# Sliding-window attention into a softplus MLP on one core: PSUM tiles of one bank in turn in place of halves of a two-bank tile, with a new hand-written opening order

## The chip, the cores and the metric

The kernel runs on one core of one Trainium2 chip. The metric is the device time of one execution in microseconds (us). It was 723.93 us before the change, the median of three runs (721.24 to 726.59).

## The reference

Attention over 4 batches, 8 heads, 768 positions of 64 dimensions, with a causal window of 128 positions and 4 positions at the start of the sequence (sinks) that all later positions see; its output feeds a two-layer MLP.

```python
scores = scale * np.matmul(q, k.transpose(0, 1, 3, 2))
keep = is_sink | in_window            # key < 4, or 0 <= query - key < 128
scores = np.where(keep, scores, -1000000000.0)
scores = scores - np.max(scores, axis=-1, keepdims=True)
a = np.exp(scores)
a = a / (np.sum(a, axis=-1, keepdims=True) + 1e-09)
out = np.matmul(a, v).astype(np.float32)
...
x = out.transpose(0, 2, 1, 3).reshape(B * S, H * D)       # 3072 x 512
h = x @ w_in                                              # w_in 512 x 2048
g = np.maximum(h, 0.0) + np.log1p(np.exp(-np.abs(h)))
return (g @ w_out).astype(np.float32)                     # w_out 2048 x 512
```

## The kernel before

**Work and tiling.** The 3072 tokens are 12 chunks of 256 (two blocks of 128 queries). For each chunk there are 8 heads of attention, and then the MLP of the chunk in 8 blocks of 256 hidden columns. The MLP of a chunk runs 8 heads behind its attention, so a steady step is one head of one chunk beside one MLP block of the chunk before it. MLP blocks are numbered over all chunks here: U9 is the second block of chunk 1, U17 the second of chunk 2, U33 the second of chunk 4. Heads likewise: S47 is the last head of chunk 5.

Chunks 0 and 1 are "exact": their heads go in pairs, in plain fp32. All later products split each operand into a high part and the rest, so that one product becomes two or three matmuls (tile names that end in h and l).

**The steps**, each a letter of the order: S scores (L245 for a pair, L260 and L261 for a head), T softmax (DVE L277 or L282 copies the diagonal, DVE L289 adds the mask and takes the maximum, ACT L290 exponentiates), N normalise (L303, L304, then L308 or L315), W transposes of the weights (PE L351 or L373, then a copy and two selections on POOL), k and K the sinks' weights (DVE L320, PE L331), V values (PE L395 and L402, or L414 and L420), O the head's output with its high part xh and rest xl (L432, L433, or L438 to L443). For the MLP: U is 24 matmuls of 128x256 (L551), F softplus in three ACT passes (L558 Abs, L559 Exp, L560 Ln), P the gate (DVE L566 reads the product in PSUM again and writes mt; then a copy to gh), R the residue (DVE, gl = mt - gh), D and E the second product, 6 matmuls each of 128x512 (L588 to L590) into the two acc tiles. The weights arrive as 64-bit words: w is the DMA of half a block (L456), a a cast of the upper word, c the assembled float (DVE L491), d its high part, l its low part (a subtraction at L67, on DVE or POOL). There are 32 halves: wi and wo for each of the 8 blocks, two halves each. L and G load q, k and v by SP's queue (L195 or L200, and L220); p and q split them; j, J and Y are the sinks of the values.

**What sets the order.** Inside `_fast` every engine runs its instructions in program order. The order is a list of tokens written by hand, `Ctx.START` (up to U9: chunks 0 and 1, the weights, the first blocks), and after it `Ctx.STEADY`, two strings of letters, one for most heads and one for the first head of a chunk. The strings `NM`, `TH`, `GH`, `WT`, `WH`, `WL` choose the engine of the n-th normalise, copy or weight step; their last letter holds for all that come later. SP's queue issues its DMAs in program order too, so an issue that waits holds all behind it.

**PSUM.** [...] Four tiles matter. `sb` (L933, two banks) holds scores: in a pair one bank for each head, later one bank for each block j. `hb` (two banks) holds the product of U: its halves, one bank each, alternate by `turn_h` (L545, L546). In chunk 0 the second block of a pair also uses it (L241). `xb` (one bank) holds values. `acc0` and `acc1` are the outputs, one bank each; one bank is for transposes. sb, hb and xb are each a single tile for the whole program, and the halves are slices of it. Waits between engines are made per tile: the framework that places them sees accesses to tiles.

Of the kernel before, what the change touches and what calls it, by code (L numbers as in the profile page):

```python
# [11 lines left out]
F32 = mybir.dt.float32  # L12
# [53 lines left out]
def _sub(nc, eng, out, a, b):  # L66
    (nc.vector if eng == "V" else nc.gpsimd).tensor_tensor(out, a, b, ALU.subtract)  # L67
# [64 lines left out]
class _Attention:  # L132
# [103 lines left out]
    def pair_scores(self, h, j):  # L236

        c, nc, chunk = self.c, self.c.nc, self.chunk
        r = self.heads.pop(h) if j else self.heads[h]
        w = KW if self.first and j == 0 else 2 * P + NS  # L240
        s = self.s[j] = c.hb if chunk == 0 and j else c.sb  # L241
        for e in range(2):
            rows = slice(e * D, e * D + D)
            q = r[rows, KC + j * P : KC + j * P + P]
            nc.tensor.matmul(s[:, e, :w], q, r[rows, j * KW : j * KW + w], start=True, stop=True)  # L245

    def scores(self, h):
        c, nc = self.c, self.c.nc
        if self.exact:
            self.pair_scores(h - h % 2, h % 2)  # L250
            return
        ops = self.heads.pop(h)
        for j in range(CH):
            s = c.sb[:, j]
            w = KW if self.first and j == 0 else 2 * P + NS
            mv = slice(j * KW, j * KW + w)
            st = slice(KC + j * P, KC + j * P + P)
            o = s[:, :w]
            hi, kl = ops
# [130 lines left out]
    def pair_values(self, h):  # L390

        c, nc, chunk = self.c, self.c.nc, self.chunk
        x = self.x[h + 1] = c.xb[:, h // 2 % 2]
        sv = c.vs[self.b, h // G][:, h % G : h % G + 2].rearrange("p g d -> p (g d)")
        nc.tensor.matmul(x, sv, self.sk[h // G], start=True, stop=False, skip_group_check=True)  # L395
        v, pts = self.v[h // 2], [self.pt.pop(h + e) for e in range(2)]
        for n in range(self.vlo, 3):
            o = slice(max(0, (n - 1) * P), min(CT, (n + 1) * P))
            m = slice(max(0, (2 * n - 1) * P), min(4 * P, (2 * n + 1) * P))
            for e in range(2):  # L400
                rows = slice(e * D, e * D + D)
                nc.tensor.matmul(  # L402
                    x[rows, o], v[:, n, rows], pts[e][:, m], start=False, stop=n == 2, skip_group_check=True
                )

    def values(self, h):
        c, nc, chunk = self.c, self.c.nc, self.chunk
        if self.exact:
            if h % 2:
                self.pair_values(h - 1)  # L410
            return
        pt, x = self.pt.pop(h), c.xb
        sv = c.vs[self.b, h // G][:, h % G]
        nc.tensor.matmul(x[:, 0], sv, self.sk[h // G], start=True, stop=False, skip_group_check=True)  # L414
        v = self.v[h // 2]
        for n in range(self.vlo, 3):
            w = v[:, n, h % 2].rearrange("p s d -> p (s d)")
            o = slice(max(0, (n - 1) * P), min(CT, (n + 1) * P))
            m = slice(max(0, (2 * n - 1) * P), min(4 * P, (2 * n + 1) * P))
            nc.tensor.matmul(x[:, :, o], w, pt[:, :, m], start=False, stop=n == 2, skip_group_check=True)  # L420
        self.x[h] = x

    def out(self, h):
        c, nc, chunk = self.c, self.c.nc, self.chunk
        r0 = (h % 2) * D
        if chunk not in c.x:
            c.x[chunk] = [c.xp.tile([P, 4, CT], F32R, tag=f"x{e}", name=f"x{e}{chunk}") for e in "hl"]
        xh, xl = c.x[chunk]
        if self.exact:
            if h % 2 == 1:  # L430
                x = self.x.pop(h)
                _copy(nc, "A", xh[:, h // 2], x)  # L432
                _sub(nc, "V", xl[:, h // 2], x, xh[:, h // 2])  # L433
# [97 lines left out]
class _Moe:  # L531
# [7 lines left out]
    def up(self, s):  # L539
        c, nc = self.c, self.c.nc  # L540
        xh, xl = c.x[self.chunk]
        if c.hb is None:
            h = c.ps_h.tile([P, 2, CT], F32, tag="h", name=f"h{self.chunk}_{s}")
        else:
            h = c.hb[:, c.turn_h].rearrange("p (j q) -> p j q", j=2)  # L545
            c.turn_h ^= 1  # L546
        prods = [(e, cc, j) for cc in range(4) for e in ("hh", "lh", "hl") for j in range(2)]
        for k, (e, cc, j) in enumerate(prods):
            wt = c.w[s, 0, cc // 2][:, "hl".index(e[0]), cc % 2, j * P : (j + 1) * P]
            x = (xh if e[1] == "h" else xl)[:, cc]  # L550
            nc.tensor.matmul(h[:, j], wt, x, start=k == 0, stop=k >= len(prods) - 2, skip_group_check=True)  # L551
        self.h[s] = h
# [49 lines left out]
def _fast(c):  # L602
# [83 lines left out]

    def idle(k):

        for _ in range(k):
            out = c.sb[:, 0, 2 * P + NS : 4 * P]  # L690
            c.nc.tensor.matmul(out, c.sk[:, :P], c.sk[:, : 2 * P - NS], start=True, stop=True, skip_group_check=True)

    parts = {
# [177 lines left out]
def _general(c):  # L871

    tc, nc = c.tc, c.nc
    c.hb = None
    with ExitStack() as st:
        pool = lambda n, bufs: st.enter_context(tc.tile_pool(name=n, bufs=bufs))
        psum = lambda n, bufs: st.enter_context(tc.tile_pool(name=n, bufs=bufs, space=bass.MemoryType.PSUM))
# [25 lines left out]
def _kernel(tc, a, out):  # L903
# [7 lines left out]
    with ExitStack() as keep:  # L911
# [24 lines left out]
        ok = nc.values_load(c.flag[:1, :1], min_val=0, max_val=1)
# [17 lines left out]
Ctx.START = """
V6 W14 V10 w S0 L8 j4 T0 S1 T1 N1 J0 S2 T2 w w w w L10 G6 G4 w w w w L12 W6 N8 S3 T3 N3 N4 w L16 W4 w S4 L14
W1 S5 w N0 T4 V0 V2 N10 a T5 S6 G8 T6 w w G10 a k0 W3 w w S8 T8 c a c N14 V4 K0 O4 a O0 V14 W12 S9 T9 W8 S7 T7
c c d W0 N5 d V8 L17 l d a l d w V1 S10 T10 w w c w V3 w l N7 O1 k4 W5 O3 a a c c d K4 a L19 N6 S11 W7 w w O10
l c G12 a d d T11 c V5 N9 a O5 N11 V7 l O7 p16 d c a O8 d d S12 l l l N2 w w U0 F0 O14 w c a U1 a W9 T12 d P0
F1 k8 S13 T13 l l c S14 T14 U2 d K8 a l c a c S15 a d V9 d P1 F2 R0 l U3 O6 c a d T15 P2 R1 l l c c p17 l w a
c a d d c w w a a l l R2 W11 N15 N13 F3 d S16 T16 D0 P3 E0 c a c k12 D1 E1 E2 a V11 G16 l D2 w w c d R3 l c d  # L960
l L18 a N16 c p19 d d U4 F4 d a S17 T17 w P4 a D3 l l E3 K12 l V12 c d R4 G14 O9 c a d U5 p18 l c l F5 W13 P5
d l D4 a O11 U6 W15 d W10 E4 W2 S18 V13 V15 N17 l a a T18 S19 c d L20 c O13 l U7 R5 O15 d D5 F6 a O2 l l P6
T19 q16 c c W16 N19 L21 U8 J16 N18 k16 p20 F7 R6 a d K16 L22 p21 G18 l d d F8 E5 c E6 S20 N12 P7 D6 T20 R7 V16
N20 O12 P8 l O16
"""


# [44 lines left out]
```

## Time and profile before

| what | value |
|---|---|
| median of three runs | 723.93 us (721.24 to 726.59) |
| the profiled execution's own time | 724.15 us |
| span of the profiled execution | 722.4 us |
| mean granted TensorE clock over the span | 0.989 |
| busy: PE, PE weight loads, DVE, ACT, POOL | 686.8, 610.1, 529.2, 475.7, 386.6 us |

The profile is one execution; its time is taken from the first to the last instruction (the span), and the execution's own time is 1.75 us longer. In the lists of waits a line names who waited, who came last, the time in total, how often, and the longest. In a timeline the two numbers ahead of an instruction are its start and its length; a matmul's length is modelled and reaches into the next one, so distances between starts tell more than ends do. "[0.40 <-DVE mt L566]" is idle time ahead of an instruction and what ended it. "x4" is a run of like instructions of which the first one's start is given. [...]

### The profile page before, as it was taken

What the parts mean: (1) busy time and instruction counts of PE and PEld (TensorE: products, weight loads), DVE (VectorE), ACT (ScalarE), POOL (GpSimd) and SP (SyncE); (2) the same over time, 40 slices, a digit from 0 to 9 for tenths busy, and PEclk for the clock granted to TensorE, in tenths of its full rate; (3) what the DMA queues carried; (4) which work ended last, traced back from release to release, by engine and by line L of the source; (5) the groups of instructions that cost most, each with busy time, mean ns of one, the idle gap of its engine ahead of it and who ended that gap; (6) DMA issues with size and microseconds to landing.
All of it is one profiled execution on the core that took longest, in us unless ns stands there. A gap on an engine that the chain in (4) does not pass through costs nothing.

```text
span 722.4 us, 13596 instructions
## 1 busy us (share of the span) xinstructions
PE 686.8 (95%) x4449; PEld 610.1 (84%) x4449; DVE 529.2 (73%) x1458; ACT 475.7 (66%) x1216; POOL 386.6 (54%) x737
## 2 busy tenths in 40 slices
PE   5689779999999999999999999999999999999996
PEld 3377668998998898998998998898998989889885
DVE  5879777877887887887788788877877777743331
ACT  6878677667666766667676776767667676754331
POOL 7572566665555564674655555675654655553110
PEclk9899999999999999999999999999999999999999
DMA  8999103221321311411321321322222321100001
GB/s 304 357 281 300 43 18 94 69 72 54 85 72 48 104 50 49 123 53 45 101 69 49 108 68 50 93 64 64 78 72 56 91 74 54 60 12 1 30 1 34
DMA packets 40051, 62.30 MB, mean 86 GB/s; under 512 B 4516, under 2 KB 21540, under 8 KB 39972
## 3 DMA queue, kind: packets, MB, share of 16 engines
q1 hardware_dynamic: 39828, 61.35, 28.1%
q8 instruction: 37, 0.61, 0.4%
q14 instruction: 42, 0.34, 0.1%
q10 hardware_dynamic: 144, 0.00, 0.0%
HBM read 55.04 MB, written 6.29 MB: 85 GB/s over the span
## 4 chain that ended last, share of the span: by engine, by line
PE 70%; ACT 13%; DVE 6%; DMA 2%; issue 2%; POOL 1%; SPq 0%; DVEq 0%; ACTq 0%; POOLq 0%
PE hb L551 33%; PE acc L588 9%; PE acc L589 9%; PE acc L590 9%; PE xb L420 4%; ACT a L290 2%; ACT mt L559 2%; ACT mt L560 2%; ACT mt L558 2%; PE sb L261 2%; PE sb L260 2%; PE t L373 2%; DVE mt L566 2%; DMA wo70r<-w 1%; PE xb L414 1%
## 5 line engine op out<-in xcount | busy, mean ns | idle before, releaser
L551 PE MATMUL hb<-xh,wi 128*128 128x256 f32 x1536 | 256.5, 290 | 10.8 <-DVE mt L566 9.4
L551 PEld LDWEIGHTS hb<-xh,wi 128*128 128x128 f32 x1536 | 212.4, 193 | 19.0 <-DVE mt L566 16.0
L551 PE MATMUL hb<-xl,wi 128*128 128x256 f32 x768 | 155.4, 284 | 0.0
L588 PE MATMUL acc<-wo,gh 128*128 128x512 f32 x384 | 153.0, 398 | 0.0
L63 POOL TENSOR_SCALAR gh<-mt 128x512 fp32r<-128x512 f32 x89 | 55.6, 625 | 181.1 <-DVE mt L566 165.4
L590 PE MATMUL acc<-wo,gl 128*128 128x512 f32 x384 | 151.2, 394 | 1.1 <-DVE gl L67 1.1
L589 PE MATMUL acc<-wo,gh 128*128 128x512 f32 x384 | 151.6, 395 | 0.0
L558 ACT ACTIVATE mt<-hb 128x512 f32<-128x512 f32 x96 | 57.4, 598 | 118.3 <-PE hb L551 117.7
L551 PEld LDWEIGHTS hb<-xl,wi 128*128 128x128 f32 x768 | 120.2, 193 | 0.0
L566 DVE SCALAR_TENSOR_TENSOR mt<-hb,mt 128x512 f32<-128x512 f32 x96 | 65.8, 685 | 48.5 <-ACT mt L560 33.4
L315 POOL TENSOR_SCALAR a<-a,rc 128x128 f32<-128x128 f32 x156 | 57.6, 381 | 64.2 <-DVE rc L304 60.6
L590 PEld LDWEIGHTS acc<-wo,gl 128*128 128x128 f32 x384 | 72.5, 189 | 18.2 <-DVE gl L67 1.5
L290 ACT ACTIVATE a<-a,stats 128x136 f32<-128x136 f32 x192 | 75.8, 396 | 14.7 <-DVE stats L289 14.6
L588 PEld LDWEIGHTS acc<-wo,gh 128*128 128x128 f32 x384 | 72.4, 189 | 12.7 <-issue 0.2
L589 PEld LDWEIGHTS acc<-wo,gh 128*128 128x128 f32 x384 | 72.6, 189 | 9.1
L67 DVE TENSOR_TENSOR gl<-mt,gh 128x512 fp32r<-128x512 f32 x96 | 69.6, 725 | 4.4 <-POOL gh L63 4.0
L560 ACT ACTIVATE mt<-mt 128x512 f32<-128x512 f32 x96 | 60.7, 633 | 3.0
L559 ACT ACTIVATE mt<-mt 128x512 f32<-128x512 f32 x96 | 60.7, 632 | 3.1
L59 ACT CAST qkh<-qk 128x656 fp32r<-128x656 f32 x80 | 59.3, 742 | 1.0 <-DMA qk<-qk 0.9
L282 DVE COPY_PREDICATED sb<-diag,sb 128x128 f32<-128x128 int32 x136 | 40.1, 295 | 25.2 <-PE sb L261 21.3
L67 DVE TENSOR_TENSOR kl<-qk,qkh 128x400 fp32r<-128x400 f32 x80 | 51.7, 647 | 2.5
L67 DVE TENSOR_TENSOR qkh<-qk,qkh 64x256 fp32r<-64x256 f32 x80 | 36.9, 462 | 17.8 <-ACT qkh L59 13.4
(190 smaller groups left out, 1204.7 us busy)
## 6 DMA issues: line engine op xcount, KB each, us to landing
qk<-qk SPq DMA_DIRECT2D x160, 164.0 KB, 3.1
vr<-v SPq DMA_DIRECT2D x32, 192.0 KB, 2.5
out<-o SPq DMA_DIRECT2D x24, 256.0 KB, 2.5
qk<-qk SPq DMA_DIRECT2D x8, 328.0 KB, 5.5
vr<-v SPq DMA_DIRECT2D x16, 128.0 KB, 2.6
wi00r<-w SPq DMA_DIRECT2D x1, 511.8 KB
wi01r<-w SPq DMA_DIRECT2D x1, 511.8 KB
wi10r<-w SPq DMA_DIRECT2D x1, 511.8 KB, 7.3
```

Source lines behind the costliest of these rows:

```text
L59: nc.scalar.copy(out, in_)
L67: (nc.vector if eng == "V" else nc.gpsimd).tensor_tensor(out, a, b, ALU.subtract)
L290: nc.scalar.activation(a, a, AF.Exp, bias=nm, scale=-1.0, accum_out=total)
L315: (nc.vector if eng == "V" else nc.gpsimd).tensor_scalar(a, a, rc[:, j : j + 1], 0.0, ALU.mult, ALU.add)
L551: nc.tensor.matmul(h[:, j], wt, x, start=k == 0, stop=k >= len(prods) - 2, skip_group_check=True)
L558: nc.scalar.activation(t[:], h[:], AF.Abs)
L559: nc.scalar.activation(t[:], t[:], AF.Exp, scale=-1.0)
L560: nc.scalar.activation(t[:], t[:], AF.Ln, bias=1.0)
L566: nc.vector.scalar_tensor_tensor(t[:], h[:], 0.0, t[:], ALU.max, ALU.add)
L588: nc.tensor.matmul(acc[:], gh[:, j, q], wh, start=f == 0, stop=False, skip_group_check=True)
L589: nc.tensor.matmul(acc[:], gh[:, j, q], wl, start=False, stop=False, skip_group_check=True)
L590: nc.tensor.matmul(acc[:], gl[:, j, q], wh, start=False, stop=f == 2 * FP - 1, skip_group_check=True)
```

## The change

The constant tiles `sb`, `hb` and `xb` go. Pairs of heads of chunks 0 and 1 take two-bank tiles from two pools of one tile each (`front_s`, `front_h`). At the first score of a single head, and at the first `up`, `follow` closes the front pool on that side and opens one in its place with two tiles of one bank (`ps_s`, tag "s"; `ps_h`, tag "h"), which are handed out in turn. The values of a pair or a head take a tile of their own from `ps_x`, which still has room for one. `out` of an even exact head returns at once. The helper `idle` is changed too, but no list holds its letter Z. START, NM, TH, GH, WT, WH and WL are new; STEADY, WM, and all that is computed stay. Lines after the change are 1 to 4 higher: U is L553, the scores are L263 and L264, the assembled weights L495, the gate L568.

```diff
-        s = self.s[j] = c.hb if chunk == 0 and j else c.sb
+        pool, tag = (c.front_h, "hb") if chunk == 0 and j else (c.front_s, "sb")
+        s = self.s[j] = pool.tile([P, 2, DM], F32, tag=tag, name=f"{tag}{chunk}_{h}_{j}")
...
-            s = c.sb[:, j]
+            if c.ps_s is None:
+                c.ps_s = c.follow("ps_s")
+            s = c.ps_s.tile([P, DM], F32, tag="s", name=f"s{self.chunk}_{h}_{j}")
...
-        x = self.x[h + 1] = c.xb[:, h // 2 % 2]
+        x = self.x[h + 1] = c.ps_x.tile([P, 2, CT], F32, tag="x", name=f"x{chunk}_{h}")[:, 0]
...
-        pt, x = self.pt.pop(h), c.xb
+        pt, x = self.pt.pop(h), c.ps_x.tile([P, 2, CT], F32, tag="x", name=f"x{chunk}_{h}")
...
-        if c.hb is None:
-            h = c.ps_h.tile([P, 2, CT], F32, tag="h", name=f"h{self.chunk}_{s}")
-        else:
-            h = c.hb[:, c.turn_h].rearrange("p (j q) -> p j q", j=2)
-            c.turn_h ^= 1
+        if c.ps_h is None:
+            c.ps_h = c.follow("ps_h")
+        h = c.ps_h.tile([P, 2, CT], F32, tag="h", name=f"h{self.chunk}_{s}")
...
+            def scores_pool(name, bufs, to):
+                side = "right" if name[-1] == "s" else "left"
+                p = tc.tile_pool(name=name, bufs=bufs, space=bass.MemoryType.PSUM, side=side, reuse_waits="tile")
+                return to.enter_context(p)
+
+            def follow(name):
+                fronts[name].close()
+                return scores_pool(name, 2, st)
...
-            c.sb, c.hb, c.turn_h = (*(p.tile([P, 2, DM], F32, name=n, bufs=1) for p, n in ((c.ps_s, "sb"), (c.ps_h, "hb"))), 0)
...
-Ctx.WL = "PPVPVPPVPPPVVPVVVVVVVPVPVVPPVPPV"
+Ctx.WL = "PPPVVPPVPPVVVPVPVPPVVVPPVPPVVPPV"
...
-l L18 a N16 c p19 d d U4 F4 d a S17 T17 w P4 a D3 l l E3 K12 l V12 c d R4 G14 O9 c a d U5 p18 l c l F5 W13 P5
-d l D4 a O11 U6 W15 d W10 E4 W2 S18 V13 V15 N17 l a a T18 S19 c d L20 c O13 l U7 R5 O15 d D5 F6 a O2 l l P6
...
+D2 P3 c a U4 L22 c l l a c d N16 R3 D3 d p17 c a p18 F4 d d V11 l l a K12 c d O11 a U5 N8 l l G18 S17 F5 c T17
+P4 c W10 l R4 p19 V13 O13 W15 a a d S18 l a U6 E3 d T18 D4 P5 d c S19 T19 R5 l l d c p20 F6 q16 l l P6 J16 N18
```

The order on the engines shows the change at three places. The first is PE at U33, the second MLP block of chunk 4, behind the values (L420) and the transposes (L373) of a head. Before:

```order
L420 MATMUL xb<-pt_0_3546,vv_0_3476 128x2x128
L373 MATMUL t_1_3637<-ident,a_0_3212 128x128 [waits PE_49]
L373 MATMUL t_1_3637<-ident,a_0_3212 128x128
L551 MATMUL hb<-xh_2856,wi_363 128x256 [waits DVE_49]
L551 MATMUL hb<-xh_2856,wi_363 128x256 x3
```

and after:

```order
L423 MATMUL x_0_3766<-pt_0_3689,vv_0_3614 128x2x128
L376 MATMUL t_1_3782<-ident,a_0_3340 128x128 [waits PE_49]
L376 MATMUL t_1_3782<-ident,a_0_3340 128x128
L553 MATMUL h_1_3794<-xh_2969,wi_385 128x256 x4
L553 MATMUL h_1_3794<-xl_2970,wi_385 128x256 x2
```

The sequence is the same, but the first matmul of the block no longer waits for DVE.

The second is PE at the scores of S47, the last head of chunk 5, followed by the second product of an MLP block. Before:

```order
L260 MATMUL sb<-qkh_7_3776 128x264 [waits Activation_49]
L261 MATMUL sb<-kl_7_3779,qkh_7_3776 128x264
L260 MATMUL sb<-qkh_7_3776 128x264
L261 MATMUL sb<-kl_7_3779,qkh_7_3776 128x264
L588 MATMUL acc_0_3798<-wo_500,gh_1_3709 128x512
```

and after:

```order
L263 MATMUL s_7_0_4030<-qkh_7_3926 128x264 [waits DVE_49,PE_49,Activation_49]
L264 MATMUL s_7_0_4030<-kl_7_3929,qkh_7_3926 128x264
L263 MATMUL s_7_1_4033<-qkh_7_3926 128x264 [waits DVE_49,PE_49]
L264 MATMUL s_7_1_4033<-kl_7_3929,qkh_7_3926 128x264
L590 MATMUL acc_0_3950<-wo_523,gh_1_3858 128x512
```

Again nothing has moved, but each of the two blocks has its own tile now, and its first matmul waits for DVE and for PE itself, where before the first waited for ACT alone. In the whole program 101 first matmuls of such blocks wait for DVE and PE together; before, none waited for PE.

The third is DVE ahead of U0, from the last weight steps to the row that U0 waits for, the last xl of chunk 0 (the second of the two here). Before:

```order
L491 SCALAR_TENSOR_TENSOR word_ps_171<-wo10r,upper_166 128x512
L304 RECIPROCAL rc_0_313<-sm_0_314 128x2x2
L308 TENSOR_TENSOR a_0_312<-a_0_312,rc_0_313 128x4x128
L67 TENSOR_TENSOR xl_332<-xb,xh_331 128x256
L304 RECIPROCAL rc_0_313<-sm_2_378 128x2x2
L67 TENSOR_TENSOR wo_424<-wt_1_0_388,wo_424 128x512
L67 TENSOR_TENSOR xl_332<-xb,xh_331 128x256
```

and after:

```order
L495 SCALAR_TENSOR_TENSOR word_ps_168<-wo10r,upper_163 128x512
L307 RECIPROCAL rc_0_389<-sm_2_457 128x2x2
L311 TENSOR_TENSOR a_0_388<-a_0_388,rc_0_389 128x4x128
L67 TENSOR_TENSOR xl_413<-x_4_493,xh_412 128x256
L495 SCALAR_TENSOR_TENSOR wt_1_1_513<-wo11r,upper_164 128x512
L67 TENSOR_TENSOR wi_518<-word_ps_167,wi_518 128x512
L495 SCALAR_TENSOR_TENSOR word_ps_167<-wi30r,upper_163 128x512
L67 TENSOR_TENSOR wo_523<-word_ps_168,wo_523 128x512
L495 SCALAR_TENSOR_TENSOR word_ps_168<-wi31r,upper_164 128x512
L67 TENSOR_TENSOR xl_413<-x_6_530,xh_412 128x256
```

Three more assembled weights (L495) and one more subtraction stand between the two xl rows. From the first DVE instruction to the second xl row DVE now does 12 assembled weights in place of 9, and 8 weight subtractions in place of 6. From U9 on, the instructions of every engine and their order are the same in both kernels.

## Rows read from the trace of the kernel before

**Rows 1.** Four stretches: length, busy PE, PEld, DVE, ACT, POOL, granted clock, DMA share, GB/s.

```profile
0.00:35.46 35.46, 21.34 (x111) 12.03 (x111) 25.23 (x98) 25.63 (x82) 21.97 (x47) 0.93 0.96 329
35.46:112.81 77.35, 65.72 (x417) 55.44 (x415) 60.16 (x139) 59.42 (x136) 43.34 (x50) 0.94 0.52 161
112.81:663.50 550.69, 547.20 (x3611) 497.67 (x3612) 427.71 (x1187) 374.21 (x973) 316.10 (x632) 1.00 0.24 67
663.50:716.20 52.70, 52.42 (x314) 44.92 (x313) 15.39 (x36) 16.44 (x27) 5.20 (x9) 1.00 0.03 11
```

**Rows 2.** PE's waits from 112.9 to 722.4 us.

```profile
PE hb L551 <- DVE mt L566: 4.4, 10, 0.9
```

**Rows 3.** PE's timeline at U33, and at U34 one head later.

```profile
279.96 0.38 PE L373 MATMUL t<-ident,a 128*128 128x128 f32 x2
280.74 0.74 PE L551 MATMUL hb<-xh,wi 128*128 128x256 f32 x4 [0.40 <-DVE mt L566]
...
287.57 0.38 PE L373 MATMUL t<-ident,a 128*128 128x128 f32 x2
287.71 0.72 PE L551 MATMUL hb<-xh,wi 128*128 128x256 f32 x4
```

**Rows 4.** DVE's timeline at U33: the gate of the block before it.

```profile
280.00 0.69 DVE L566 SCALAR_TENSOR_TENSOR mt<-hb,mt 128x512 f32<-128x512 f32 x1 [0.25 <-ACT mt L560]
```

**Rows 5.** PE's timeline at U94, in the tail that has MLP blocks alone.

```profile
698.60 0.39 PE L590 MATMUL acc<-wo,gl 128*128 128x512 f32 x1
699.04 0.74 PE L551 MATMUL hb<-xh,wi 128*128 128x256 f32 x4
```

**Rows 6.** PE's waits from 0 to 112.9 us, four of twelve lines.

```profile
PE hb L551 <- DVE mt L566: 5.9, 4, 2.7
...
PE ts L331 <- DVE sa L320: 2.3, 1, 2.3
...
PE acc L590 <- DVE gl L67: 1.1, 1, 1.1
...
PE hb L551 <- ACT mt L558: 0.7, 1, 0.7
```

**Rows 7.** The chain that ended last, around U2 and U6: start, length, what.

```profile
46.30 3.14 PE hb L551 x24
...
81.80 0.61 DVE mt L566
...
82.45 4.45 PE hb L551 x24
```

**Rows 8.** DVE's line L491 in the first two stretches: length, busy, count, clock.

```profile
0.00:35.46 35.46, 6.33 (x9) 0.93 0.96 329
35.46:112.81 77.35, 19.54 (x23) 0.94 0.52 161
```

**Rows 9.** Groups up to 112.8 us: weight subtractions on POOL and on DVE.

```profile
L67 POOL TENSOR_TENSOR wi<-wt,wi 128x512 fp32r<-128x512 f32 x7 | 10.4, 1487 | 2.1 <-ACT wi L59 1.9
...
L67 DVE TENSOR_TENSOR wi<-wt,wi 128x512 fp32r<-128x512 f32 x6 | 4.1, 682 | 0.0
```

**Rows 10.** Timelines of DVE and of POOL near 100 us, one row each.

```profile
100.15 1.33 DVE L491 SCALAR_TENSOR_TENSOR wt<-wo70r,upper 128x512 int32<-128x512 int32 x1
...
99.63 1.30 POOL L67 TENSOR_TENSOR wo<-wt,wo 128x512 fp32r<-128x512 f32 x1 [4.11 <-ACT wo L59]
```

**Rows 11.** PE's timeline ahead of the values of V19, whose first matmul waits for two engines.

```profile
131.08 0.40 PE L589 MATMUL acc<-wo,gh 128*128 128x512 f32 x1
131.32 0.39 PE L590 MATMUL acc<-wo,gl 128*128 128x512 f32 x1
131.55 0.28 PE L414 MATMUL xb<-sk,vs 128*128 128x256 f32 x1
```

**Rows 12.** The weight half wi61: its transfer in the chain, its cast in ACT's timeline.

```profile
52.46 6.16 DMA wi61r<-w
...
68.84 0.78 ACT L59 CAST upper<-wi61r 128x512 f16<-128x512 bf16 x1
```

More of the change, by code (lines that the diff above doesn't have):

```diff
@@ L425, in out @@
         r0 = (h % 2) * D
+        if self.exact and h % 2 == 0:
+            return
         if chunk not in c.x:
@@ L429, in out @@
         if self.exact:
[L430 to L433, printed above, removed]
+            x = self.x.pop(h)
+            _copy(nc, "A", xh[:, h // 2], x)
+            _sub(nc, "V", xl[:, h // 2], x, xh[:, h // 2])
             return
@@ L687, in idle @@
     def idle(k):
-        for _ in range(k):
-            out = c.sb[:, 0, 2 * P + NS : 4 * P]
+        if c.idle is None:
+            c.idle = c.ps_acc.tile([P, DM], F32, tag="acc0", name="idle")
+        for _ in range(k if moe[0].acc is None else 0):
+            out = c.idle[:, : 2 * P - NS]
             c.nc.tensor.matmul(out, c.sk[:, :P], c.sk[:, : 2 * P - NS], start=True, stop=True, skip_group_check=True)
@@ L873, in _general @@
     tc, nc = c.tc, c.nc
-    c.hb = None
     with ExitStack() as st:
@@ L928, in _kernel @@
             c.lp, c.ap, c.sp = pool("lp", 2), pool("ap", 2), pool("sp", 2)
-            c.ps_acc, c.ps_h = psum("ps_acc", 1), psum("ps_h", 1)
-            c.ps_s, c.ps_t, c.ps_x = psum("ps_s", 1), psum("ps_t", 1), psum("ps_x", 1)
-            c.xb = c.ps_x.tile([P, 2, CT], F32, name="xb")
+            c.ps_acc, c.ps_t, c.ps_x = psum("ps_acc", 1), psum("ps_t", 1), psum("ps_x", 1)
+            fronts = {}
+            def scores_pool(name, bufs, to):
[5 more added lines that the diff above has]
+                return scores_pool(name, 2, st)
+            for n in ("ps_s", "ps_h"):
+                fronts[n] = st.enter_context(ExitStack())
+            c.front_s, c.front_h = (scores_pool(f"front{n[2:]}", 1, own) for n, own in fronts.items())
+            c.follow, c.ps_s, c.ps_h, c.idle = follow, None, None, None
             c.xf = c.sp.tile([P, 2, CT], F32, name="xf", bufs=1)
-            c.sb, c.hb, c.turn_h = (*(p.tile([P, 2, DM], F32, name=n, bufs=1) for p, n in ((c.ps_s, "sb"), (c.ps_h, "hb"))), 0)
             with tc.manual_schedule(engines=ORDERED):
@@ L942 @@
 Ctx.GB, Ctx.EXACT = 3, 2
-Ctx.NM = "PPPPPVPVPAPPPPPAPAPPAPPP"
-Ctx.TH = "VAVVAAAAAAVAAAVAVAAAA"
-Ctx.GH = "PAAAAPAAAPPP"
+Ctx.NM = "PPPPPAPPPAPAPPPVPAPPAPPPP"
+Ctx.TH = "VVVAAAAAAAVAAAVAAAAAAA"
+Ctx.GH = "PAAAAAVVVPPPP"
 Ctx.WM = "sssssssppsppssssssssssssssssssss"
-Ctx.WT = "PAAAAAAAAAAAAPPPAAAAAAAAPAAAAAAV"
-Ctx.WH = "PAAAVPAAAPPAPAAAAAAAAAAAPAPPPAAA"
-Ctx.WL = "PPVPVPPVPPPVVPVVVVVVVPVPVVPPVPPV"
+Ctx.WT = "AAVAAAAAAAAAAAAPPAAAAAAAAAAAAAAV"
+Ctx.WH = "APPPAAPAPPPPAAVAPAPAVAAVPAAAVAPA"
+Ctx.WL = "PPPVVPPVPPVVVPVPVPPVVVPPVPPVVPPV"
 Ctx.STEADY = (
@@ L954 @@
 Ctx.START = """
[L955 to L960, printed above, removed]
-l L18 a N16 c p19 d d U4 F4 d a S17 T17 w P4 a D3 l l E3 K12 l V12 c d R4 G14 O9 c a d U5 p18 l c l F5 W13 P5
-d l D4 a O11 U6 W15 d W10 E4 W2 S18 V13 V15 N17 l a a T18 S19 c d L20 c O13 l U7 R5 O15 d D5 F6 a O2 l l P6
-T19 q16 c c W16 N19 L21 U8 J16 N18 k16 p20 F7 R6 a d K16 L22 p21 G18 l d d F8 E5 c E6 S20 N12 P7 D6 T20 R7 V16
-N20 O12 P8 l O16
+W0 N12 V14 V4 O4 V6 V0 S0 N6 V12 w j4 V2 N14 W14 O0 V10 N0 w w L8 O2 N2 S1 J0 w w w L10 L12 w T0 T1 S2 G4 w V8
+N1 w w w G8 w w G6 T2 L16 w w w w w G10 w L14 w G12 w w w w w L18 S3 T3 N3 L17 w w w S4 T4 w W1 w k0 a a S5 T5
+c c W12 w w W8 d K0 d a S6 T6 c l l S7 W3 a O6 O8 S8 T7 d l O12 T8 c O14 d V1 N5 N7 O1 a a c d S9 T9 c N9 k4 a
+W5 V3 a S10 T10 l c c O3 S11 d K4 a a T11 l c N11 O10 l V5 O5 W7 S12 c a d d l l c d l d a c V7 O7 N4 a k8 c l
+p16 d d a W9 U0 F0 U1 T12 c a a d P0 S13 T13 c R0 c d d K8 G14 N13 a F1 a U2 F2 l l l V9 S14 P1 l W11 W4 T14
+G16 c l c W2 D0 a d S15 d P2 l L19 U3 a L20 T15 W13 R1 E0 c l S16 c N15 D1 O9 E1 k12 R2 E2 F3 d l d d a a T16
+D2 P3 c a U4 L22 c l l a c d N16 R3 D3 d p17 c a p18 F4 d d V11 l l a K12 c d O11 a U5 N8 l l G18 S17 F5 c T17
+P4 c W10 l R4 p19 V13 O13 W15 a a d S18 l a U6 E3 d T18 D4 P5 d c S19 T19 R5 l l d c p20 F6 q16 l l P6 J16 N18
+W16 E4 V15 a O15 U7 N19 S20 c c c U8 D5 E5 F7 N17 k16 N10 T20 R6 F8 P7 R7 P8 K16 E6 d d d L21 p21 a D6 N20 V16
+W6 l l O16
 """
```

## The prediction, made before the changed kernel ran

> **What bounds the kernel now.** I read the busy time by stretches first, then PE's waits before and after 112.9 us, then timelines around single waits, and the chain that ended last. The stretches [rows 1] show two kernels in one. From 112.81 to 716.2 us PE is the bound: 547.2 busy of 550.7 us, then 52.4 of 52.7, at a granted clock of 1.00. Little can be won there, and only where PE stands still. The opening is different: to 35.46 us, where the first MLP block U0 starts, PE is busy 21.3 us and the transfers fill the DMA engines (0.96); from there to 112.81 us, where U9 starts, it is busy 65.7 of 77.35 us at a clock of 0.94. DVE and ACT carry 60 us each there, so PE, DVE and ACT take turns in holding the others.
>
> PE's waits after 112.9 us are a single line [rows 2]: U waits for the gate, ten times, 4.4 us. The longest, 0.9 us, is U9's, which the view before 112.9 us counts too; nine are left, all at the second block of a chunk. The wait is not for data: U33's product goes into the other half of hb than the gate reads. As hb is one tile, the reader of one bank holds the writer of the other. The gate of the block before it starts at 280.00 and lasts 0.69; U33 starts at 280.74, right behind it [rows 3, 4].
>
> **The change, part by part.** Durations come from the profiled execution, so the sum starts from its 724.15 us (0.2 above the median of the runs).
>
> *The nine waits of the steady part.* With two tiles in turn, U33 needs only the gate before the previous one, and its order row has lost the wait for DVE. From the transposes to U33 it is 0.78 us from start to start (279.96 to 280.74), at U34 without a wait 0.14 [rows 3]: 0.64 is lost. The idle column gives 0.40 for it, as it counts from a modelled end; the difference is 0.24. The idle of the nine is 4.4 - 0.9 = 3.5 us, and nine times 0.24 makes 5.7. PE is the bound here, so all of it should come out: **-5.7**. Next in line is ACT's softplus, and a block's D and E follow more than a head later, so nothing near is late. Below nothing it can't fall: the sequence is unchanged. It could be less if a wait turns up at D instead; I keep -5.7 as the upper and the lower value, and put the doubt into a rival.
>
> *The tail.* U89 to U95 stand behind E alone. U94 starts 0.44 after the last matmul of E [rows 5]; without a wait the next matmul starts 0.23 after such a row [rows 11]. Seven times 0.21: **-1.5**.
>
> *The opening's waits of U.* The same false wait costs 5.9 us in four (U5, U6, U8, U9; the longest, 2.7, at U6) and 0.7 at U1, which waits for U0's Abs [rows 6]: 6.6 us. U6 starts at 82.45, when the gate P5 that began at 81.80 has ended [rows 7]. In the new list P4 stands behind U5 and P5 behind U6, which the old tile would not have allowed without a loss. Here PE is not the only bound, so the gain lies between 0 and 6.6. I take **-6.6**, because in this stretch no other engine is busy over 78% [rows 1] and the nearest row, the longest wait, stands alone in the chain ahead of U6.
>
> *The clock.* At 0.94 over 77.35 us, with two levels of 1 and 0.5, some 12% or 9.3 us ran at the lower one; at the higher that work takes 4.6 us less. U6, right behind its wait of 2.7 us, took 4.45 us for 24 matmuls, U2 3.14 [rows 7], so fewer holes should give part of it back. Bounds 0 and -4.6; I take **-2.0**, somewhat more than U6's own 1.3.
>
> *More work ahead of U0.* The order of DVE shows 12 assembled weights in place of 9 ahead of the last xl of chunk 0, which U0 needs, and 8 weight subtractions in place of 6. At 6.33 / 9 = 0.70 us [rows 8] and 0.68 us [rows 9] that is 3 x 0.70 + 2 x 0.68 = 3.5 us. DVE is idle 10.2 of the first 35.46 us [rows 1], so a part goes into its holes. Bounds 0 and +3.5; as DVE is busy 71% of that stretch, I take **+2.0**. The work is not lost, later DVE has it behind it.
>
> *The rest of the new list.* From U0 to U9 the new order could remove also the waits for the sinks' weights (2.3) and for the residue (1.1) [rows 6], or bring them at other places. I take 0 and keep -3.4 for the range. Of SP's queue: the value load of chunk 1's third pair of heads, which has to wait until an earlier load's buffer is read, now stands ahead of 12 weight halves, before of 9. Three halves of 128 x 512 words of 8 bytes, 0.52 MB each, at 329 GB/s [rows 1] are 4.8 us of transfers that may begin later. The first half behind the load, wi61, landed at 58.62 before and was cast at 68.84 [rows 12]: 10 us of cover, so I cost it at 0; without the cover, the 4.8 us would delay the casts and with them U6 and U7.
>
> *The new waits.* 101 first matmuls of a block of scores now wait for DVE and for PE's own earlier work. What they wait for is two tiles back and long done. The nearest row is V19, whose first matmul waits for two engines: it starts 0.23 us after the matmul ahead of it, which itself started 0.24 after its forerunner [rows 11]. So a met wait costs nothing there, and I take 0. If each did hold PE for such a step, it would be 101 x 0.23 = 23.2 us. [...]
>
> The sum: -5.7 - 1.5 - 6.6 - 2.0 + 2.0 = -13.8, so 724.15 - 13.8 = **710.4 us**.
>
> **The rivals.**
>
> *B, the opening gives nothing.* There, a wait that is removed only uncovers the next: DVE, ACT and POOL are at 78, 77 and 56% [rows 1]. The new strings also give POOL 16 weight subtractions in place of 13, at 1.49 us each against 0.68 on DVE [rows 9], and in the new order U5 waits for POOL. For it speaks that the gain needs three engines to fall into step; against it, that the gate waits were a PE-only hold, and that the longest stands in the chain. Only the steady part and the tail gain: 724.15 - 7.2 = 717.0 us; with U0 late by 3.5, 720.5. A slower DVE belongs here. An assembled weight took 1.33 us beside a POOL subtraction of 1.30 [rows 10], against 0.70 in the first stretch [rows 8]: 0.63 more, and three more POOL subtractions may cost DVE 1.9 us. [...]
>
> *C, the new waits hold PE.* Place: the first matmul of both score blocks in each head, on PE, the bound. Price: up to 0.23 us each, 23.2 us in all, which gives 724.15 - 13.8 + 23.2 = 733.6 us, slower. It decides from 13.8 / 101 = 0.14 us a wait. Against it stands V19.
>
> *D, the change doesn't do what it says.* The tiles of one pool could still be held by each other's readers. Then the 13.8 shrink to the later U0: 724.15 + 2.0 = 726.2 us at the worst. Against it: U33's row in the new order has no wait at all.
>
> **How the numbers follow.** The forecast, 710.4, has a chance of 0.70; B, about 717 to 720.5, has 0.21; C 0.06; D 0.03. The low end takes U0 not late (-2.0), the whole clock (-2.6 more) and the two other waits gone (-3.4): 702.4, and I put 702.0. The high end is B's, 720.5; C and D above it are 9 in 100. Within 1% means 7.2 us, about what a measurement of this kernel can tell from no change. Faster by more than that, below 716.7, is the forecast: 0.70. Within it are B and D: 0.24. Slower is C: 0.06.
>
> **What would show it.** Right: after U9 no line of PE waiting for the gate; U33 0.14 us behind its transposes; U9 to the end 7.2 us shorter than 722.4 - 112.8 = 609.6 us; U0 at about 37.5 us, and U9 at about 106 us. U6 without a hole ahead of it, in about 3 us. Wrong for B: U9 at 113 to 116 us, with new waits of PE for POOL's or DVE's wi in place of the gate. Wrong for C: a gap of 0.1 us or more ahead of L263 in every steady head, and a steady head longer than before. For D: the line of hb and the gate is still there. If the steady part gains and U9 is late, the opening's step was wrong; if U9 is early and the end is not, the steady one.

## The result and the profile after

The changed kernel takes 706.01 us, the median of four runs (703.99 to 706.80), against 724.46 for the kernel before in the same comparison: a ratio of 0.9745, with a 95% interval of 0.9701 to 0.9788. The forecast was 710.4 in a range of 702.0 to 720.5. The profiled span fell by 17.3 us, from 722.4 to 705.1.

The four stretches of the changed kernel, cut at the same events as [rows 1]: the starts of U0, U9 and U88, and the end of the last product.

```profile
0.00:36.52 36.52, 25.68 (x114) 13.77 (x115) 26.84 (x99) 27.07 (x83) 24.85 (x50) 0.91 0.97 337
36.52:101.89 65.37, 60.49 (x414) 51.18 (x413) 59.95 (x139) 55.74 (x131) 35.79 (x44) 1.00 0.57 175
101.89:648.20 546.31, 545.01 (x3614) 497.30 (x3613) 423.20 (x1189) 374.70 (x973) 322.15 (x637) 1.00 0.24 68
648.20:698.90 50.70, 50.70 (x314) 45.35 (x313) 15.38 (x36) 16.50 (x27) 5.20 (x9) 1.00 0.03 11
```

Where PE is the bound the two last rows are 4.4 and 2.0 us shorter than in [rows 1], and PE has next to no idle time left. The second row shows the opening: PE's idle time fell from 77.35 - 65.72 = 11.6 us to 65.37 - 60.49 = 4.9, and its busy time by 5.2 us, as the granted clock rose from 0.94 to 1.00. The clock records of both profiles have two values only, 1.00 and 0.50; 106.0 to 109.3 us of the kernel before, for one, was granted 0.50. Not all of the 5.2 is the clock. The new list puts W9, four transposes of weights, ahead of U0; in the kernel before it stood behind U1 and took 0.6 us:

```profile
43.21 0.60 PE L351 MATMUL t<-ident,a 128*128 128x128 f32 x4
```

PE's waits of the changed kernel, from U0 to U9 and then from 102 us to the end:

```profile
PE s L263 <- DVE stats L292: 3.4, 1, 3.4
PE h L553 <- DVE xl L67: 0.6, 1, 0.6
PE acc L592 <- DVE gl L67: 0.5, 1, 0.5
PE x L417 <- DVE sk L67: 0.4, 1, 0.4
...
PE x L423 <- POOL pt L388: 1.3, 1, 1.3
```

Both lines of U that waited for the gate and for Abs are gone, in the opening [rows 6] and after it [rows 2]. New are above all two: 3.4 us ahead of a block of scores (S19), and 1.3 us at V17. The timelines of PE and DVE at U33, and of PE at U94:

```profile
269.34 0.38 PE L376 MATMUL t<-ident,a 128*128 128x128 f32 x2
269.47 0.72 PE L553 MATMUL h<-xh,wi 128*128 128x256 f32 x4
...
269.09 0.69 DVE L568 SCALAR_TENSOR_TENSOR mt<-h,mt 128x512 f32<-128x512 f32 x1 [0.25 <-ACT mt L562]
...
681.83 0.39 PE L592 MATMUL acc<-wo,gl 128*128 128x512 f32 x1
682.06 0.52 PE L553 MATMUL h<-xh,wi 128*128 128x256 f32 x3
```

U33 starts 0.13 us behind the transposes, where it was 0.78 [rows 3], while the gate of the block before it is still running (269.09 to 269.78): the bank that the gate reads no longer holds the other (a bank is half of the kernel's [P, 2, DM] tile, 512 floats in a partition). U94 starts 0.23 behind E, where it was 0.44 [rows 5].

Where the 17.3 us came from, by the starts of the blocks in the timelines of both profiled executions:

| stretch | before | after | change | forecast |
|---|---|---|---|---|
| start to U0 | 35.46 | 36.52 | +1.06 | +2.0 |
| U0 to U9 | 77.35 | 65.37 | -11.98 | -8.6 |
| U9 to U16 | 49.06 | 50.60 | +1.54 | 0 |
| U16 to U88 (the nine waits) | 501.67 | 495.75 | -5.92 | -5.7 |
| U88 to U95 (the tail) | 41.43 | 39.44 | -1.99 | -1.5 |

### The profile page after: what moved, and what is told of

Read it like the earlier page. It is cut to its first block, busy times and chain, and to the rows that moved or that the text cites. A ratio compares the mean times of both kernels' runs of the same rounds, so it can differ in the third digit from the quotient of the medians.

```text
span 705.1 us, 13714 instructions
## 1 busy us (share of the span) xinstructions
PE 681.9 (97%) x4449; PEld 607.6 (86%) x4449; DVE 526.1 (75%) x1461; ACT 474.0 (67%) x1213; POOL 388.0 (55%) x737
## 4 chain that ended last, share of the span: by engine, by line
PE 86%; DMA 6%; POOL 3%; issue 3%; ACT 1%; SPq 0%; DVE 0%; POOLq 0%; DVEq 0%; ACTq 0%
PE h L553 36%; PE acc L590 12%; PE acc L591 12%; PE acc L592 12%; PE x L423 5%; PE s L263 3%; PE s L264 3%; PE t L376 2%; DMA wo50r<-w 2%; PE x L417 1%; DMA wi31r<-w 1%; DMA wo30r<-w 1%; DMA wo60r<-w 1%; DMA words<-sizes 1%; DMA vsr<-vs 1%
## 5 line engine op out<-in xcount | busy, mean ns | idle before, releaser
L553 PE MATMUL h<-xh,wi 128*128 128x256 f32 x1536 | 253.2, 287 | 0.0
L553 PEld LDWEIGHTS h<-xh,wi 128*128 128x128 f32 x1536 | 211.0, 191 | 1.3 <-issue 0.5
L553 PE MATMUL h<-xl,wi 128*128 128x256 f32 x768 | 154.7, 283 | 0.6 <-DVE xl L67 0.6
L560 ACT ACTIVATE mt<-h 128x512 f32<-128x512 f32 x96 | 57.4, 598 | 104.7 <-PE h L553 104.2
L553 PEld LDWEIGHTS h<-xl,wi 128*128 128x128 f32 x768 | 119.3, 191 | 0.8 <-DVE xl L67 0.8
L568 DVE SCALAR_TENSOR_TENSOR mt<-h,mt 128x512 f32<-128x512 f32 x96 | 66.0, 687 | 42.7 <-ACT mt L562 29.7
L67 DVE TENSOR_TENSOR gl<-mt,gh 128x512 fp32r<-128x512 f32 x96 | 73.9, 770 | 4.4 <-POOL gh L63 4.0
L443 DVE TENSOR_TENSOR xt<-x,xt 64x256 f32<-64x256 f32 x80 | 33.2, 415 | 28.5 <-ACT xt L59 27.8
```

The source lines that it names most:

```text
L560: nc.scalar.activation(t[:], h[:], AF.Abs)
L568: nc.vector.scalar_tensor_tensor(t[:], h[:], 0.0, t[:], ALU.max, ALU.add)
```

## The experiments

All were timed beside the kernel before, in five rounds.

| kernel | median us | ratio to before (95%) | U0, U9 in its profile |
|---|---|---|---|
| U's tiles alone, old list | 706.06 | 0.9741 (0.9728 to 0.9754) | 37.42, 101.00 |
| new list and strings alone | 729.15 | 1.0067 (1.0047 to 1.0087) | 36.27, 117.15 |
| changed, constant score tile | 702.87 | 0.9704 (0.9691 to 0.9717) | 37.25, 99.86 |
| U's and score tiles, old list | 704.35 | 0.9723 (0.9710 to 0.9735) | 36.71, 100.80 |
| changed, once more | 705.09 | 0.9723 (0.9708 to 0.9738) | 36.56, 103.52 |
| changed, G12 moved | 702.81 | 0.9701 (0.9688 to 0.9713) | 35.86, 98.55 |
| the same, constant score tile | 703.44 | 0.9711 (0.9698 to 0.9723) | 36.66, 99.42 |
| before, holes filled | 723.81 | 0.9984 (0.9973 to 0.9995) | 36.43, 112.34 |
| G12 moved, old WL | 708.82 | 0.9776 (0.9760 to 0.9792) | 39.03, 103.77 |
| G12 moved, old WT, WH, WL | 713.08 | 0.9828 (0.9811 to 0.9845) | 43.47, 109.15 |
| G12 moved, once more | 703.24 | 0.9695 (0.9679 to 0.9711) | 36.47, 97.93 |

### U's tiles alone, with the old list

```diff
-            h = c.hb[:, c.turn_h].rearrange("p (j q) -> p j q", j=2)
-            c.turn_h ^= 1
+        if c.ps_h is None:
+            c.ps_h = c.follow("ps_h")
+        h = c.ps_h.tile([P, 2, CT], F32, tag="h", name=f"h{self.chunk}_{s}")
```

(with `front_h` for chunk 0 and the pool of two as in the change; all else as before)

> The kernel before with one edit: U takes tiles of one bank in turn from a pool of two; scores, values, list and strings stay as before. Theory (the hold of one two-bank tile is the cost): U17 to U88 gain 5.9 us and the tail 2.0, as in the changed kernel, and in the opening the waits of U for the gate (5.9 in four) and for Abs (0.7) go, most of them for good: U9 at 106 to 109 in place of 112.8, total 709 to 713 us. Rival (the opening's gain is the new list's): the opening's waits only change their name, U9 at 111 to 113, total 715 to 717 us.

Measured: 706.06 us, better than the theory's own range. PE's waits from 36.5 us on, all of them:

```profile
PE sb L245 <- DVE stats L289: 1.1, 1, 1.1
PE h L549 <- POOL wi L67: 1.0, 2, 0.7
PE xb L420 <- POOL pt L385: 0.8, 2, 0.6
PE ts L331 <- DVE sa L320: 0.2, 1, 0.2
```

and its stretch from U0 to U9:

```profile
37.42:101.00 63.58, 61.10 (x417) 51.97 (x416) 57.02 (x136) 57.56 (x131) 41.21 (x48) 1.00 0.59 183
```

This edit gives what the whole change gives, in the opening too: U0 to U9 takes 63.58 us in place of 77.35, 1.8 less than with the new list. Not only U's own waits went: the wait for the sinks' weights (2.3) is 0.2, and the one for the residue (1.1) is gone; by what path the edit removed these two was not followed. PE is busy 61.1 of 63.6 us, so it is the bound there too, and the clock is at 1.00. As the list is the old one, the matmuls from U0 to U9 are those of [rows 1]: PE's busy time for the same work fell from 65.72 to 61.10, by 4.6 us. The rival, a gain of the list, falls.

### The new list and strings alone, with the old tiles

```diff
-Ctx.NM = "PPPPPVPVPAPPPPPAPAPPAPPP"
+Ctx.NM = "PPPPPAPPPAPAPPPVPAPPAPPPP"
...
-Ctx.WL = "PPVPVPPVPPPVVPVVVVVVVPVPVVPPVPPV"
+Ctx.WL = "PPPVVPPVPPVVVPVPVPPVVVPPVPPVVPPV"
```

(before, with START, NM, TH, GH, WT, WH and WL of the change)

> The kernel before with the new list and strings, and its constant two-bank tiles. Theory: the nine waits at the chunks' second blocks and the seven of the tail are back (0 gained after U9), and in the opening the gates that now stand behind the next U are held too, so U5 to U9 wait more than in the changed kernel: U9 at 108 to 116, total 720 to 728 us. Rival (the list makes the opening faster by itself): U9 at 102 to 105, total 714 to 717 us.

Measured: 729.15 us, slower than before. PE's waits from 36.5 to 118 us, the first two of six lines, and from 117.3 us on:

```profile
PE hb L551 <- DVE mt L566: 5.2, 2, 3.4
PE hb L551 <- ACT mt L558: 4.9, 2, 3.5
...
PE hb L551 <- DVE mt L566: 3.4, 9, 0.5
```

The nine waits are back, and in the opening the list pays for the hold with 10.1 us. These waits stand at U1 and U2, which follow the softplus of the block before, and at U3 and U7, which follow a gate; the longest two are U2's and U7's:

```profile
50.79 0.36 PE L551 MATMUL hb<-xh,wi 128*128 128x256 f32 x1 [3.50 <-ACT mt L558]
...
98.69 0.74 PE L551 MATMUL hb<-xh,wi 128*128 128x256 f32 x4 [3.40 <-DVE mt L566]
```

U5 and U6, which the new list puts ahead of gates, did not wait. New list and old tiles lose 4.9 us, new tiles and old list win 18: the list is no gain by itself. With the new tiles the sign is not clear: the new list is 1.7 us behind with the score tiles in turn (706.01 against 704.35) and 3.2 ahead with the constant one (702.87 against 706.06). Either is small beside the 18 us of U's tiles.

### The score tiles

```diff
-            if c.ps_s is None:
-                c.ps_s = c.follow("ps_s")
-            s = c.ps_s.tile([P, DM], F32, tag="s", name=f"s{self.chunk}_{h}_{j}")
+            s = c.sb[:, j]
```

(one kernel: the change, with `c.sb` as one constant two-bank tile again, pairs too; the other: before, with U's and the score tiles of the change, values and list as before)

> The changed kernel with one part undone: scores in one constant two-bank tile, as before, so that the 101 first matmuls of a block lose their double waits. Theory: the waits are met and cost nothing, and the turn of score tiles brings nothing: the same as the changed kernel, 705 to 707 us. [...] Rival (the turn of score tiles brings part of the gain): longer by 2 us or more, with new waits of PE for DVE ahead of the scores.

> The kernel before with the new tiles for U and for scores (front pools and followers), the old constant tile for values, the old list and strings. Theory: as U's tiles alone, within 1.5 us. Rival: the score tiles bring or cost something of their own, 2 us or more apart from U's tiles alone.

Measured: 702.87 us without the tiles in turn, 3 below the changed kernel; with the old list, 704.35 with them, 1.7 below U's tiles alone. The signs differ, so neither is a cost of the double waits. That cost is read where both kernels run the same order. U11 and U88 of the changed kernel, and then of the one with the constant score tile:

```profile
117.32 0.48 PE L553 MATMUL h<-xh,wi 128*128 128x256 f32 x2
...
648.24 0.40 PE L553 MATMUL h<-xh,wi 128*128 128x256 f32 x2
```

```profile
114.79 0.48 PE L550 MATMUL h<-xh,wi 128*128 128x256 f32 x2
...
645.62 0.40 PE L550 MATMUL h<-xh,wi 128*128 128x256 f32 x2
```

530.92 us with the double waits, 530.83 without: 0.09 us over 73 heads. The prediction's rival C, with up to 0.23 us a wait, is dead. The 3 us lie in the opening: S19 starts at 84.66 in the changed kernel and at 82.06 here. Why S19 waits is the next experiment; with that wait out of both, the score tiles in turn are 0.6 us ahead (702.81 against 703.44, below). What they bring, 0.6 to 1.7 us, was not followed further, and 0.6 is little beside the 0.7 to 4.9 us by which executions of one kernel differ here.

### The late transfer: G12 moved

In the changed kernel, S19's 3.4 us is, by the waits of its profile, the end of a chain. DVE's `stats` of head 18 are late, as DVE's split of head 19 stands ahead of them and waits 3.73 us for ACT, and ACT for a q and k transfer. The rows of DVE's and ACT's timelines, and one of SP's waits:

```profile
81.25 0.42 DVE L67 TENSOR_TENSOR qkh<-qk,qkh 64x256 fp32r<-64x256 f32 x1 [3.73 <-ACT qkh L59]
...
80.47 0.74 ACT L59 CAST qkh<-qk 128x656 fp32r<-128x656 f32 x1 [4.50 <-DMA qk<-qk]
```

```profile
SPq L220 <- PE x L405: 12.1, 1, 12.1
```

G12, the load of values of which the prediction spoke, waits 12.1 us on SP's queue for its buffer (it was 5.2 us before). The DMA engines' throughput from 40 to 84 us in 40 slices, of the changed kernel:

```profile
GB/s 410 310 91 11 0 0 0 15 6 277 331 220 335 320 368 391 354 173 227 176 259 226 235 328 406 402 413 402 405 345 273 196 179 129 71 33 26 0 0 7
```

They run dry from 43 to 49 us, and the weights behind G12 land until about 78 us; head 19's q and k, issued at 70.6 behind them, are there when ACT starts at 80.47. The wait of G12 alone does not make the transfer late. In the kernel with the constant score tile, which has the same list, G12 waited even longer and the engines ran dry as well, but then they moved more (349 GB/s from 59 to 69 us in place of 276) and were done by about 77 us; S19 did not wait. The same two views of it:

```profile
SPq L220 <- PE x L402: 13.1, 1, 13.1
GB/s 398 338 126 11 0 0 0 0 15 64 289 234 339 342 275 406 424 344 227 276 267 395 413 409 387 409 413 406 221 277 154 265 243 24 0 0 0 122 191 0
```

So, as far as these profiles show, the 3 us between the two kernels came from how fast the weights behind G12 moved; why that differed is open. The experiment moves one token:

```diff
-... w L14 w G12 w w w w w L18 ... c c W12 w w W8 d ...
+... w L14 w w w w w w L18 ... c c W12 w w G12 W8 d ...
```

> The changed kernel as it is, for the three others on the same chip: 703.5 to 706.5 us, with the wait of PE ahead of the scores of head 19 for a late q and k transfer (3.4 us in its profile) back in part or whole.

> The changed kernel with one token moved: the value load G12 behind the last weight transfer, no longer ahead of 12 halves. Theory (SP's queue: the load waits 12 us for a buffer, the DMA engines run dry from 43 to 49 us, the weights end 6 us late, and the q and k load of head 19 behind them lands 9 us after its issue and holds PE for 3.4 us): no dry stretch, the weights landed by about 72 us, PE's wait ahead of head 19 under 0.5 us, U9 at 98 to 100 in place of 101.9, total 701.5 to 704 us. Rival (the late landing was chance, or another wait takes its place): the same as the changed kernel within 1 us.

> The changed kernel with the constant two-bank tile for scores and with G12 behind the last weight transfer. Theory (score tiles cost nothing, and the 3 us between the changed kernel and the one with the constant score tile were the late transfer): the same as G12 moved alone within 1 us. Rival (the score tiles cost 2 us or more in the opening): 2 us or more below it.

The changed kernel, once more: 705.09 us. In its profiled execution, the slowest of the five (708.22 us), S19 waits 2.6 us, and behind this hole the clock fell, as it had not in the first profile:

```profile
PE s L263 <- DVE stats L292: 2.6, 1, 2.6
...
86.50:90.00 3.50, 3.50 (x12) 2.28 (x12) 3.50 (x11) 3.47 (x12) 1.51 (x1) 0.51 0.00 0
```

Measured, with G12 moved: 702.81 us (702.54 to 703.22) against 705.09 (703.33 to 708.22) on the same chip; with the constant score tile 703.44. The same DMA line and PE's waits from U0 to U9, all of them:

```profile
GB/s 420 411 397 417 409 413 413 320 236 183 239 257 281 372 417 417 413 409 402 334 149 54 0 0 0 0 0 39 189 245 253 262 10 0 0 0 172 134 0 0
```

```profile
PE h L553 <- DVE xl L67: 1.2, 1, 1.2
PE x L423 <- POOL pt L388: 0.9, 1, 0.9
PE acc L592 <- DVE gl L67: 0.5, 1, 0.5
```

No dry stretch, the weights landed by 64 us, PE's wait gone, U9 at 98.55. The theory holds with the numbers that it gave (only the weights landed earlier still than the 72 us expected), and this version beats both kernels; once more, it took 703.24 us. The changed kernel's runs on that chip lay 4.9 us apart, these 0.7, which speaks for the late transfer, with the clock of 0.51 that the profile shows behind its hole, as what made them differ; the unprofiled runs can't show it.

### The kernel before, with its holes filled

```diff
-d l D4 a O11 U6 ...
+d l D4 Z18 a O11 U6 ...
...
-... U8 J16 N18 k16 ...
+... U8 Z16 J16 N18 k16 ...
```

(Z is `idle`: matmuls of 128x248 whose output nobody reads; they are work beside the reference's)

> The kernel before with 18 matmuls of 128x248 that nobody reads ahead of U6 and 16 behind U8, in the two long holes of PE. Theory (the holes bring the lower clock behind them, 82.5 to 85.8 and 106 to 109 us): both stretches at 1.00, U6 in about 3.1 us in place of 4.45, U9 2 to 3.5 us earlier, total 720.5 to 722.5 us. Rival (the clock falls whatever stands there, or other engines take up what PE gains): the same as before within 1 us.

Measured: 723.81 us, a ratio of 0.9984. The stretches 81 to 87 and 105 to 110 us, of the kernel before, then of this one:

```profile
81.00:87.00 6.00, 4.55 (x27) 4.55 (x28) 2.76 (x5) 1.50 (x4) 2.74 (x3) 0.72 0.23 67
105.00:110.00 5.00, 5.00 (x19) 4.11 (x17) 3.96 (x9) 4.19 (x8) 4.92 (x10) 0.66 0.49 128
```

```profile
81.00:87.00 6.00, 5.38 (x47) 5.18 (x46) 3.96 (x7) 2.69 (x6) 2.75 (x3) 1.00 0.22 67
105.00:110.00 5.00, 5.00 (x28) 4.16 (x26) 4.79 (x14) 4.41 (x9) 4.92 (x10) 1.00 0.46 131
```

Here, in the profiled execution, the two stretches were granted 1.00 in place of 0.72 and 0.66, and U6 took 2.97 us (83.69 to the transposes at 86.66) in place of 4.29 (82.45 to 86.74). But U0 to U9 gained only 77.35 - 75.91 = 1.4 us, U9 came 0.5 earlier where 2 to 3.5 were expected, and the total gained 0.6, as the second half of the rival has it. The PE that is faster waits longer for the gates, which still hold it: U9's wait grew from 0.94 to 2.07 us. Nor is the clock at 1.00 in the whole stretch; it is lower behind U0's start still.

```profile
112.34 0.74 PE L551 MATMUL hb<-xh,wi 128*128 128x256 f32 x4 [2.07 <-DVE mt L566]
...
36.43:112.34 75.91, 67.02 (x452) 57.13 (x450) 60.95 (x139) 59.45 (x136) 43.03 (x50) 0.98 0.50 158
```

### The strings of the weights

```diff
-Ctx.WL = "PPPVVPPVPPVVVPVPVPPVVVPPVPPVVPPV"
+Ctx.WL = "PPVPVPPVPPPVVPVVVVVVVPVPVVPPVPPV"
```

(the change with G12 moved, and with WL of before; then with WT and WH of before, too)

> The changed kernel with G12 moved, and with the string WL of before, which puts 13 of the weight subtractions on POOL in place of 16 (3 more of 0.68 us on DVE, 3 less of 1.49 on POOL). Theory (POOL's subtractions slow DVE's assembled weights, but U to U9 have cover): the 32 assembled weights take 1 to 3 us less DVE time than the 29.4 us with G12 moved, the total within 1 us of it, 702 to 704 us. Rival (POOL is what holds the opening in the new list): 1.5 us or more faster. Rival (DVE holds it, so 3 more subtractions cost): 1.5 us or more slower.

> The changed kernel with G12 moved, and with all three weight strings of before (WT, WH, WL). Theory (order and strings were fitted to each other and either alone moves the opening by little): 702 to 706 us, any loss as new waits of PE for wi ahead of U2 to U7. Rival (the strings carry the new list): slower by 4 us or more.

> The changed kernel with G12 moved, for the two others on the same chip: 702 to 703.5 us.

Measured: 708.82 and 713.08 us against 703.24, so 5.6 and 9.8 us slower; both theories, which gave at most 1 us to WL and 706 us to all three strings, fall. U0 starts at 39.03 and 43.47 in place of 36.47. With the old WL the number of subtractions on DVE ahead of U0 is the same, only the third and the fourth weight half swap engines; the third one's high part comes from POOL, and DVE, which runs in order, waits for it. DVE's waits from 10 to 40 us, first line:

```profile
DVE wi L67 <- POOL wi L63: 3.0, 1, 3.0
```

With the new WL this line is not there. So ahead of U0 it is the place of a step that goes with the loss, not the number of steps. That is 2.6 of the 5.6 us; another 3.3 arise from U0 to U9, with the old WL and then with the new one:

```profile
39.03:103.77 64.74, 61.32 (x414) 51.31 (x413) 62.15 (x142) 56.02 (x131) 33.63 (x41) 1.00 0.50 161
36.47:97.93 61.46, 59.81 (x414) 51.21 (x412) 60.20 (x140) 55.76 (x131) 37.69 (x44) 1.00 0.56 186
```

There DVE has three more subtractions, the rival's cause; which of its steps held PE was not followed, nor was the loss with all three strings, whose profile does not show the 3.0 us. The 32 assembled weights did get faster, 28.8 us against 29.6, less than the 1 to 3 expected.

## Why the prediction was right

**The steady waits and the tail** were right in cause, place and size: -5.9 for -5.7, and -2.0 for -1.5. U's tiles alone have all of it, the list alone none.

**The opening's waits of U.** PE's idle time from U0 to U9 fell by 6.7 us, for the forecast's "I take -6.6", but by two misses that cancel, which is luck: the wait for the sinks' weights (2.3) and half of the residue's (1.1, now 0.5), costed at 0, went as well, and 3.4 came back at S19. That the new list puts gates behind the next U was no reason: the old list with the new tiles gains more, and the new list with the old tiles loses. B, that a removed wait only uncovers the next, was wrong the other way: more waits went with it. D falls too, as the line of hb and the gate is gone.

**The clock** was the mis-sized term: "I take -2.0", and for the same work PE's busy time fell by 4.6 us (U's tiles alone), the whole of the bound, which was taken for an end that is hardly reached. In the changed kernel it fell by 5.2, of which 0.6 is W9, now ahead of U0; the prediction did not count it. Two things stand behind the 4.6. With the holes filled but the waits kept, a clock of 0.98 in place of 0.94 made the stretch only 1.4 us shorter; with the waits gone, PE is busy 96% of it (61.1 of 63.6), and nearly every microsecond of clock counts. And not all of the lower clock came from holes behind U0: before, 2.2 us of it lay right behind U0's start, and in the changed kernel it ends ahead of U0. The first row is of the kernel before, the second of the changed one:

```profile
35.46:37.70 2.24, 2.24 (x12) 2.24 (x11) 2.18 (x4) 1.54 (x3) 0.48 (x1) 0.51 0.78 303
28.50:35.40 6.90, 6.11 (x22) 3.12 (x24) 5.25 (x14) 5.45 (x15) 3.07 (x5) 0.51 1.05 295
```

At half the clock, 2.2 us are some 1.1 of the 4.6, which no wait of U gave.

**U0** came 1.1 us later for the 2.0 forecast, but with the old list it came at 37.42 and 36.71, too, and at 36.43 in the kernel before with its holes filled, whose order up to U0 is unchanged. So a microsecond here is what executions differ by, and can't be put down to the new list's extra DVE work. That DVE can hold U0 is made likely by the strings: a wait of 3.0 us on DVE goes with a U0 that is 2.6 us later.

**SP's queue** was the step that failed: "10 us of cover, so I cost it at 0". wi61 had its cover (it was cast at 64.45 us, earlier than before), and the three halves that G12 now stands ahead of did start later, by 3.9 to 9.4 us where 4.8 were estimated. What was late was the transfer behind the weights, head 19's q and k, which the prediction did not look at. It cost 3.4 us in the profile, and moving G12 gained 2.3 in the medians. Where the weights moved faster, with the constant score tile, the same wait of G12 cost nothing. Another give-back, 1.3 us of PE behind POOL at V17, was not foreseen either.

**The double waits** cost nothing, as taken from V19's row [rows 11]: 530.92 us with them and 530.83 without, 0.09 us over 73 heads, where C had up to 23.2.

**Slower DVE** (under B): the 32 assembled weights took 25.9 us of DVE before [rows 8] and 29.6 after, 3.8 us more where 1.9 was estimated:

```profile
0.00:36.52 36.52, 8.75 (x11) 0.91 0.97 337
36.52:101.89 65.37, 20.89 (x22) 1.00 0.57 175
```

One of them took 1.33 us beside a POOL subtraction of 1.30, against a mean of 0.70 in the first stretch [rows 8, 10]; what makes them slower no run shows. The number of POOL subtractions, from which the 1.9 were estimated, is at most 0.8 of the 3.8: with the old WL, and so 13 of them again, the 32 took 28.8. And it did not set the end: the order with more of them on POOL is the faster one, 703.24 us against 708.82.

So the sum was 3.5 us short of the 17.3: the clock by 2.6, W9 by 0.6, the opening's waits by 0.1, U0 by 0.9, and the steady part and the tail by 0.7, less the 1.5 given back after U9 that was not in it.

## What to carry to other kernels

Two halves of one tile are one thing to whoever places the waits: if one engine fills a half while another reads the other, give each its own tile, and look in the trace for a wait whose releaser touches other bytes than the waiter. A token list and the tiles that it was fitted to have to be judged in all four combinations: here U's tiles with the old list have the whole gain, and the list with the old tiles loses. When a load on an in-order queue waits for a buffer, ask for every transfer behind it when it is needed, the last ones above all.

## What the runs showed of the hardware that was not expected

The clock. In the kernel before, PE stood idle for 2.69 us ahead of U6, and the stretch 81 to 87 us was granted 0.72. In the changed kernel PE stood idle for 3.41 us ahead of S19, from the matmuls of D4 on, and the same stretch was granted 1.00:

```profile
81.00:87.00 6.00, 2.59 (x15) 2.11 (x14) 5.59 (x19) 5.80 (x15) 4.33 (x4) 1.00 0.22 57
```

With the longer hole the stretch was granted 1.00, with the shorter one 0.72. It is not the kernel that decides either: in the second profile of the changed kernel, with a hole of 2.64 us at the same place, the stretch 86.5 to 90 us was granted 0.51, where the first profile has 1.00:

```profile
86.50:90.00 3.50, 3.50 (x30) 2.77 (x29) 3.44 (x10) 3.44 (x9) 0.59 (x1) 1.00 0.00 0
```

So one order of matmuls met both clocks in two executions, and PE's busy time from U0 to U9 was 1.4 us longer in the second (61.85 against 60.49). What decides it was not tried.
